# ScalarE issues the weights' transfers into ten slots, v is split and loaded a head sooner with its maximum pinned, and heads take even shares of the queued products

## The chip, the cores and the metric

One NeuronCore of a Trainium2 chip runs the whole program. TensorE (PE) multiplies, PEld is its weight load, VectorE (DVE) and ScalarE (ACT) do the elementwise work, GpSimd (POOL) helps them, SyncE (SP) issues transfers. All of them run in their own order and wait for each other through semaphores. The metric is the device time of one execution in microseconds (us); lower is better.

## The reference

Eight batches of eight attention heads with a decay on the scores, then a two-layer product with a hard swish between (`_attn_ref`, `_moe_ref`, cut):

```python
scores = (1/8) * q @ k.T                       # q, k, v: 8 x 8 x 576 x 64
cum = cumsum(log(clip(f, 1e-4, 1)))
scores = where(causal, -1e9, scores + cum[:, None] - cum[None, :])
attn = exp(scores - max); attn = attn / (sum(attn) + 1e-9)
x = (attn @ v), heads side by side             # 4608 x 512
h = x @ w_in                                   # w_in: 512 x 2048
out = (h * clip(h + 3, 0, 6) / 6) @ w_out      # w_out: 2048 x 512
```

The weights come as 64-bit floats; the kernel reads them as pairs of 32-bit integers.

## The kernel before

**Heads.** The list VH holds the order of the attention work: four A entries (two heads each, the first 256 rows of batch 0), eight B entries (the other rows of batch 0, one head each), then 56 F entries (one head each, batches 1 to 7). In A and B the scores are exponentiated into `pf` (L567); in F each row's maximum is taken by DVE (`pp` and `MF`, L619), ACT exponentiates (L631) and splits into two f16 parts in `ring`, and a transposing transfer brings them into `pT`. `av` multiplies by v into `pav`; `x_move` transposes the result into `xT`.

**Products.** A tile is 512 rows of x. `h_unit` makes `ph` (L781 to L783, three f16 products for one precise one) and from it, over `r` (ACT L791, DVE L794), `gT` (L795, L796). `out_unit` makes `po` (L803 to L805) and stores `o`. These units stand in a list, `units`; `done` appends a tile when its last head is done, and `fill`, called eight times a head, takes units off it as long as its credit lasts. The credit grows by `rates[0]`: 0.6 in B, 0.45 in batch 1, 1.02 in later batches. One tile costs about 64 credits.

**Weights.** Each of w_in and w_out comes in 16 chunks of 512 KB. A chunk is loaded into a slot (`w_load`, L237, on SP's queue), decoded into f32 (`w_decode`: ACT L250, DVE L251 and L252) and its squares summed (ACT L256); the slot is then free. After that a scale is made and the chunk is split into two f16 parts: w_in over ACT L283, TensorE (`low`, L286 and L287) and ACT L288, w_out over ACT L283 and DVE L294. w_in uses up to six slots (three `ring` buffers, three in the unused end of `w2`), five chunks ahead; w_out uses the three `ring` buffers. `both` takes the decoding of w_in and then of w_out in steps, W_RATE of them a head.

**v.** The f32 copy `vst` of one batch's v is loaded in three transfers (`load_v`, L359 and L360), its largest magnitude is reduced on DVE in two halves (`vm`, L365, in `v_scale`), a scale follows, and `v_split` makes the f16 parts of two heads at a time (ACT L396, DVE L397). The load of the next batch comes at head 6 of a batch, the maximum at head 7, the splits of a batch at head 7 of the one before and at heads 1, 3 and 5.

**Order.** The layer below the kernel (Tile) puts the instructions of each engine into one fixed order, from the order of the code and its own timeline of the program; only `tc.keep_in_program_order` and `tc.issue_after` bind it. On the chip each engine runs its order and waits at the first instruction whose semaphores are not there. A transfer announces its landing on one of eight semaphores (DMAHW0 to DMAHW7) which all transfers of the program take in turn, whichever engine issues them; a transfer waits until the one eight places before it has landed, so eight at most are under way.

Of the kernel before, what the change touches and what calls it, by code (L numbers as in the profile page):

```python
# [13 lines left out]
I32 = mybir.dt.int32  # L14
# [6 lines left out]
def kernel(  # L21
# [10 lines left out]
    nc = tc.nc  # L32
# [13 lines left out]
    NFC = DFF // P  # L46
    TT = 512
# [34 lines left out]
    NQK, NL, NST = 3, 2, 3  # L82
    W_RATE = (8, 5, 4)
    H_COST = 1.05
    F_RATE = (0.6, 0.45, 1.02)
    PIN = 0
    PIN0 = 1
    LOW_W = 0
    W_GAP = 5
# [5 lines left out]
    QA = 256  # L95
    CA = QA // P
    VH = [("A", g) for g in range(NPAIR)] + [("B", n) for n in range(H)]
# [3 lines left out]
    NSP = 3  # L101
    PL_POOL = ((3, ), ())
    NAT = ((1, 4, 0), (2, 3))
    B0_POOL = ((0, 0), (1, 1))
    W_AHEAD = (4, 5)
    W_ORDER = 0
    POOL_REST = ((0, 0, 0, 0), (0, 0, 0, 0))
    PIN_V = 1
# [22 lines left out]
    vst = cpool.tile([P, NCH, VR], F32, name="vst")  # L131
# [4 lines left out]
    xT = [cpool.tile([P, NCC, 2, TT // P, 2, 64], F16, name=f"xT{i}") for i in range(3)]  # L136
# [7 lines left out]
    def v_parts(b):  # L144
        return v0 if b == 0 else [vst[:, 0:3], vst[:, 3:]]
# [86 lines left out]

    def w_load(i, k, slots):
        src, x, _ = w_chunk(i, k)
        with pinned() if PIN or i == 0 and k < 8 else nullcontext():
            if wide:
                nc.sync.dma_start(slots[k % len(slots)], src.bitcast(I32))  # L237
            else:
                nc.sync.dma_start(x, src)

    def w_decode(i, k, slots):

# [51 lines left out]
            nc.vector.scalar_tensor_tensor(lo, x, sc, hi, op0=ALU.mult, op1=ALU.subtract)  # L294

    def w_in_work():
        first, ahead = W_AHEAD
        for k in range(first):
            w_load(0, k, slots_in)
        yield  # L300
        for k in range(first, ahead):
            w_load(0, k, slots_in)
        for j in range(NG):
            ks = range(j * NCC, (j + 1) * NCC)
            for k in ks:
                if k + ahead < NW:
                    w_load(0, k + ahead, slots_in)
                w_decode(0, k, slots_in)
                yield
            pm = w_gram(ks) if GRAM[j] else w_sum(ks[0], ks[-1] + 1)  # L310
            yield
            yield from pow2_scale(pm, S1 + j, I1 + j, f"w0{j}")
            eye = None
            if PE_LOW[j]:
                eye = p2.tile([P, DM], F32, tag="o", name=f"eye{j}")[:, 0:P]
                nc.vector.tensor_scalar(
                    eye, identf, scol(S1 + j), -1.0, op0=ALU.mult, op1=ALU.mult
                )
            for k in ks:
                w_split(0, k, scol(S1 + j), eye)  # L320
                yield
            w_in_done.append(j)

    def w_out_work():
        n = len(slots_out)
        for k in range(n):
            w_load(1, k, slots_out)
        yield

        for k in range(NW):  # L330
# [13 lines left out]
        for k in range(NW):
            w_split(1, k, scol(SW2 + k // NG))
            yield


    def load_v(b):
        src = vS[b]  # L350
        lo, hi = v_parts(b)
        with pinned() if PIN_V else nullcontext():
            if b == 0:
                nc.sync.dma_start(lo, src[0:3 * P].rearrange("(c p) e -> p c e", p=P))
                nc.sync.dma_start(hi[:, 0], src[3 * P:4 * P])
                nc.sync.dma_start(hi[:64, 1], src[4 * P:S])
            else:
                for p in (0, 64):
                    nc.sync.dma_start(vst[p:p + 64, 0], src[0:64])  # L359
                nc.sync.dma_start(vst[:, 1:], src[64:].rearrange("(c p) e -> p c e", p=P))  # L360

    def v_scale(b):
        pm = p2.tile([P, 2], F32, tag="pm", name=f"vm{b}")
        for i, t in enumerate(v_parts(b)):
            nc.vector.tensor_reduce(  # L365
                pm[:, i:i + 1], t.rearrange("p c (h e) -> p (c h) e", e=D + 1)[:, :, 0:D],
                axis=AX.XY, op=ALU.max, apply_absolute_value=True,
            )
# [466 lines left out]
    dec = decay()  # L835
    w_in_q = w_in_work()
    w_out_q = w_out_work()
    w_in_done = []

    def both():  # L840
        yield from w_in_q
# [34 lines left out]

    units = []

    credit, rates = [0.0], [1.0]

    def w_step():
        with tc.high_priority(offset=-LOW_W):
# [2 lines left out]
    def fill(k):  # L885
        credit[0] += k * rates[0]
        while credit[0] >= 1 and units:
            with tc.high_priority(offset=-LOW_M):
                r = next(units[0], 0)
            if r == 0:  # L890
                units.pop(0)
            else:
                credit[0] -= r
        credit[0] = min(credit[0], 1.0)

    def one(*a):
        yield from moe_tile(*a)

    def done(v):
        kind, n = VH[v]  # L900
        if kind == "A":
            if n == NPAIR - 1:
                units.append(one(0, 0, QA))
            return
        b, h = divmod(n, H)
        if h == H - 1:
            units.append(one(b, QA if b == 0 else 0, TT))
            if b == B - 1:
                units.append(one(B))

    prev = None
    pend_x = None
    vq = v_scale(0)
    for i, (kind, n) in enumerate(VH):
        b, h = divmod(n, H)
        if kind == "A":
            b = h = 0
        wn = W_RATE["ABF".index(kind)]
        rates[0] = F_RATE[0] if kind == "B" else F_RATE[min(b, 2)]
        ahead = i + 2 < NV  # L920
        if i + 3 < NV:
            load_x(i + 3)
        if ahead:
            load_c(i + 2)
# [24 lines left out]
        fill(1)  # L949
        if pend_x is not None:  # L950
            x_move(pend_x)
            done(pend_x)
            pend_x = None
        if front:
            natural(i + 2, 0)
# [18 lines left out]
            v_split(n // 2)  # L974
        fill(1)
        prev = (i, ph)
    rates[0] = 1.0
    av(*prev)
    fill(4)
# [40 lines left out]
```

## Time and profile before

| | |
|---|---|
| median of three runs | 1084.57 us (1083.75 to 1087.27) |
| the profiled execution | 1083.28 us, its span 1081.5 us |
| PE busy | 1010.1 us, 93% of the span |
| DVE, ACT, POOL busy | 719.7, 610.1, 413.1 us |
| TensorE clock granted, mean | 0.982 |
| transfers | 133.74 MB, 124 GB/s in the mean |

Five stages can be told by ACT's exponentials: A (to 65.2 us, where the first B head's exponential starts), B (to 133.1 us, where the last one's second half starts), the first F heads with the splits of w_out (to 190 us), the rest of batch 1 and the start of batch 2 (to 290 us), batches 2 to 7 (to 893 us), and last the products that are left. In the rows of the profile a number, a duration, an engine and a line stand first, then written tile, arrow, read tile; in brackets is the idle time of the engine before it and what ended that.

### The profile page before, as it was taken

How to read it: one execution, taken by the hardware profiler on the slowest of the kernel's cores; microseconds unless marked ns; L12 is line 12 of the kernel's file. 1: busy time of each engine (PE TensorE's matmuls, PEld its weight loads, DVE VectorE, ACT ScalarE, POOL GpSimd, SP SyncE). 2: the span in 40 equal slices, each digit the busy share in tenths (PEclk: the TensorE clock that was granted, in tenths of full speed). 3: DMA queues.
4: the chain of work that ended last, by engine and by line, in shares of the span. 5: the costliest groups of instructions: out<-in, count | busy, mean ns of one | idle time of the engine just before them, and what ended most of it. 6: DMA issues, size and time to landing. Idle time of an engine off the chain costs nothing.

```text
span 1081.5 us, 20281 instructions
## 1 busy us (share of the span) xinstructions
PE 1010.1 (93%) x7074; PEld 577.4 (53%) x7074; DVE 719.7 (67%) x1887; ACT 610.1 (56%) x1285; POOL 413.1 (38%) x505
## 2 busy tenths in 40 slices
PE   2799977988999999999999989999999999999998
PEld 2567854755555555555555545555555555444443
DVE  7869899876885688468865795689668841510520
ACT  4778656845764577356754674477447841621520
POOL 7344455335434445444544444454445420000000
PEclk9989989999999999999999999999999999999999
DMA  8866547767756666667576856675666651000001
GB/s 258 277 172 194 150 105 134 179 127 150 156 114 141 140 146 118 137 129 164 108 139 138 164 113 130 146 166 114 128 140 128 106 112 46 1 10 30 1 1 39
DMA packets 261650, 133.74 MB, mean 124 GB/s; under 512 B 229444, under 2 KB 231036, under 8 KB 261548
## 3 DMA queue, kind: packets, MB, share of 16 engines
q1 hardware_dynamic: 261548, 132.45, 54.7%
q8 instruction: 56, 0.92, 0.3%
q14 instruction: 46, 0.38, 0.1%
HBM read 47.93 MB, written 9.73 MB: 53 GB/s over the span
## 4 chain that ended last, share of the span: by engine, by line
PE 64%; DVE 12%; DMA 9%; issue 5%; ACT 5%; SPq 2%; POOL 2%; DVEq 0%; POOLq 0%; ACTq 0%
PE po L803 10%; PE po L804 10%; PE po L805 10%; PE ph L781 7%; PE ph L782 7%; PE ph L783 7%; DMA vst<-in_vS_dram 3%; PE pn L611 3%; PE pn L608 2%; DVE pp L619 2%; DVE ring L648 2%; DMA T<-TK 1%; DVE gT L796 1%; DMA w<-in_w_in_dram 1%; DVE r L794 1%
## 5 line engine op out<-in xcount | busy, mean ns | idle before, releaser
L781 PE MATMUL ph<-xT,w 128*128 128x512 f16 (+1 forms) x640 | 231.2, 363 | 14.5 <-DVE r L794 9.1
L782 PE MATMUL ph<-xT,w 128*128 128x512 f16 (+1 forms) x640 | 230.2, 363 | 0.0
L783 PE MATMUL ph<-xT,w 128*128 128x512 f16 (+1 forms) x640 | 230.0, 363 | 0.0
L631 ACT ACTIVATE pp<-pp,nb 128x192 f32<-128x192 f32 x280 | 138.5, 552 | 148.8 <-DVE nb L625 145.8
L804 PE MATMUL po<-w,gT 128*128 128x512 f16 x576 | 216.3, 381 | 6.1 <-DVE w L294 6.1
L805 PE MATMUL po<-w,gT 128*128 128x512 f16 x576 | 215.9, 381 | 0.0
L803 PE MATMUL po<-w,gT 128*128 128x512 f16 x576 | 213.6, 381 | 1.1 <-ACT o L814 0.8
L648 DVE TENSOR_TENSOR ring<-pp,ring 128x128 f16<-128x128 f32 (+2 forms) x216 | 131.5, 622 | 84.1 <-ACT ring L645 83.2
L791 ACT ACTIVATE r<-ph,bias_r,SC 128x256 f32<-128x256 f32 (+7 forms) x272 | 144.4, 570 | 28.6 <-PE ph L783 27.9
L794 DVE SCALAR_TENSOR_TENSOR r<-r,ph 128x512 f32<-128x512 f32 (+1 forms) x160 | 100.1, 627 | 88.9 <-ACT r L791 88.6
L458 POOL TENSOR_TENSOR T<-ST,T 64x576 fp32r<-64x576 f32 (+1 forms) x68 | 101.2, 1488 | 143.2 <-DMA T<-TK 133.4
L619 DVE CUSTOM_DVE_ANT_0 pp<-pn,W 128x192 f32<-128x192 f32 x280 | 122.9, 482 | 20.6 <-PE pn L611 16.6
L796 DVE TENSOR_TENSOR gT<-r,gT 128x512 f16<-128x512 f32 (+1 forms) x160 | 118.3, 743 | 27.4 <-ACT gT L795 26.6
L795 ACT CAST gT<-r 128x512 f16<-128x512 f32 (+1 forms) x160 | 91.8, 575 | 75.9 <-DVE r L794 75.8
L608 PE MATMUL pn<-TK,TQ 68*128 68x192 f32 x336 | 124.1, 383 | 5.8 <-issue 5.0
L611 PE MATMUL pn<-T,T 128*128 128x192 f32 x336 | 113.5, 368 | 4.3 <-POOL T L458 4.3
L645 ACT CAST ring<-pp 128x192 f16<-128x192 f32 x280 | 112.9, 452 | 0.0
L455 POOL TENSOR_TENSOR T<-ST,TQ 64x576 fp32r<-64x576 f32 (+2 forms) x68 | 97.6, 1435 | 24.8 <-PE pn L611 18.2
L654 POOL TENSOR_TENSOR ring<-pp,ring 128x128 f16<-128x128 f32 x96 | 61.5, 641 | 105.5 <-ACT ring L645 83.7
L782 PEld LDWEIGHTS <-w 128*128 128x128 f16 x640 | 62.7, 99 | 65.8 <-issue 20.9
L805 PEld LDWEIGHTS <-gT 128*128 128x128 f16 x576 | 56.8, 99 | 74.9 <-issue 13.7
L781 PEld LDWEIGHTS <-w 128*128 128x128 f16 x640 | 63.1, 99 | 62.2 <-issue 14.3
(136 smaller groups left out, 1703.4 us busy)
## 6 DMA issues: line engine op xcount, KB each, us to landing
ST<-in_qk_dram SPq DMA_DIRECT2D x64, 288.0 KB
T<-TK SPq DMA_DIRECT2D x64, 144.0 KB
out_dram<-o SPq DMA_DIRECT2D x36, 256.0 KB
ring<-in_w_out_dram SPq DMA_DIRECT2D x16, 512.0 KB
T<-TQ SPq DMA_DIRECT2D x56, 144.0 KB
vst<-in_vS_dram SPq DMA_DIRECT2D x7, 1040.0 KB
ring<-in_w_in_dram SPq DMA_DIRECT2D x9, 512.0 KB
w<-in_w_in_dram SPq DMA_DIRECT2D x7, 512.0 KB
```

Of the source, the lines that this page charges most:

```text
L608: nc.tensor.matmul(dst, TQ[i][0:D + 4, qs], TK[i][0:D + 4, a:e], start=True, stop=False)
L611: nc.tensor.matmul(dst, T7[j][:, qs], T1[j][:, a:e], start=False, stop=True)
L619: nc.vector.tensor_tensor_reduce(pp[:r, w:w + kw], pn[:r, o:o + kw], W[:r, 4 * P + r - kw:4 * P + r], 1.0, -3.0e38, ALU.add, ALU.max, accu ...
L631: nc.scalar.activation(x_, x_, AF.Exp, bias=nb[:r, e0 + x:e0 + x + 1], scale=0.125)
L648: eng.tensor_tensor(hl[:r, a:a + c * P], pp[:r, at[c] + 64:at[c] + kw], hl[:r, h0[c] + 64:h0[c] + kw], op=ALU.subtract,)
L781: nc.tensor.matmul(ph, w1[0][:, cc, fs_], xh, start=(cc == 0), stop=False)
L782: nc.tensor.matmul(ph, w1[0][:, cc, fs_], xl, start=False, stop=False)
L783: nc.tensor.matmul(ph, w1[1][:, cc, fs_], xh, start=False, stop=(cc == NCC - 1))
L791: nc.scalar.activation(r[:, a:e], ph[:, a:e], AF.Relu, bias=bias_r, scale=scol(A1 + NG * b + fc * NG // NFC))
L803: nc.tensor.matmul(po, gT[:, 0, fc, ts_], w2[:, fc, 0, :], start=(fc == 0), stop=False)
L804: nc.tensor.matmul(po, gT[:, 0, fc, ts_], w2[:, fc, 1, :], start=False, stop=False)
L805: nc.tensor.matmul(po, gT[:, 1, fc, ts_], w2[:, fc, 0, :], start=False, stop=(fc == NFC - 1))
```

## The change

`w_load` issues on ScalarE's queue instead of SP's, without pinning. The slots of w_out grow from three to five (two halves of `vst`), those of w_in from six to ten (these five, two in `xT[1]`, three in `w2`), and w_in is loaded as many chunks ahead as there are slots. `load_v` of later batches moves from head 6 to head 5, and `v_split` from heads 1, 3, 5 to 1, 2, 4; the maximum of later batches is kept in program order. A batch's tile enters the list one step later (`moved`). From batch 2 on the rate is no constant: `even` spreads the credits that are left, less a reserve of 8, over the heads until the next tile comes.

```diff
-    F_RATE = (0.6, 0.45, 1.02)
+    F_RATE = (0.6, 0.45)
-    W_AHEAD = (4, 5)
-    slots_out = [t[:, :] for t in ring]
-    slots_in = slots_out + [spare[:, (2 * h + 9) * CW:(2 * h + 11) * CW] for h in range(NSP)]
+    slots_out = [t[:, :] for t in ring] + [vsp[:, 2 * h * CW:2 * (h + 1) * CW] for h in range(2)]
+    slots_in = slots_out + [xsp[:, 2 * h * CW:2 * (h + 1) * CW] for h in range(2)]
+    slots_in += [spare[:, (2 * h + 9) * CW:(2 * h + 11) * CW] for h in range(NSP)]
 def w_load(i, k, slots):
-        with pinned() if PIN or i == 0 and k < 8 else nullcontext():
-                nc.sync.dma_start(slots[k % len(slots)], src.bitcast(I32))
+            nc.scalar.dma_start(slots[k % len(slots)], src.bitcast(I32))
 def w_in_work():
-        first, ahead = W_AHEAD
+        ahead = len(slots_in)
...
+                w_decode(0, k, slots_in)
                 if k + ahead < NW:
                     w_load(0, k + ahead, slots_in)
-                w_decode(0, k, slots_in)
 def v_scale(b):
-            nc.vector.tensor_reduce(
+            most = nc.vector.tensor_reduce(
...
+            if b:
+                tc.keep_in_program_order(most)
...
+    TILE = NFC * 2 * H_COST + TT // P * NFC // 2 * (2.0 - H_COST)
+    RESERVE = 8.0
+    def even(h):
+        heads = (1 - h) % H + 1
+        return min(max((left[0] - RESERVE) / (8 * heads), 0.5), 1.25)
...
-        rates[0] = F_RATE[0] if kind == "B" else F_RATE[min(b, 2)]
-        if b + 1 < B and h == 6:
+        if b and h in (1, 2, 4):
+            v_split(n // 2 + 1 if h > 1 else (n + 1) // 2)
+        if b + 1 < B and h == (5 if b else 6):
             load_v(b + 1)
-        if b and h % 2 == 1 and h < H - 1:
-            v_split((n + 1) // 2)
+        if moved is not None:
+            done(moved)
+            moved = None
+        rates[0] = F_RATE[0] if kind == "B" else F_RATE[b] if b < 2 else even(h)
...
             x_move(pend_x)
-            done(pend_x)
+            if VH[pend_x][0] == "F":
+                moved = pend_x
+            else:
+                done(pend_x)
```

The lines of the new code stand a few lines lower (L250 is L251 there, L567 is L570, L365 is L366).

**ACT at the start of the program.** `lf` is the logarithm from which the decay `cs` is made, `gT`, `ring`, `vst`, `xT` and `w` hold the slots or the decoded chunks. Before:

```order
L161 ACT_TABLE_LOAD
L161 ACTIVATE warm<-warm 1x1
L169 ACTIVATE lf<-fs 64x576
L170 ACT_TABLE_LOAD
L170 ACTIVATE warm<-lf 1x1
L250 ACTIVATE gT<-ring_123 128x512
```

Now, with the semaphores that each waits for:

```order
L238 DMA vst<-in_w_in_dram 128x1024
L238 DMA vst<-in_w_in_dram 128x1024 [waits DMAHW0_49]
L238 DMA xT_118<-in_w_in_dram 128x1024 [waits DMAHW1_49]
L238 DMA xT_118<-in_w_in_dram 128x1024 [waits DMAHW2_49]
L238 DMA w_115<-in_w_in_dram 128x1024 [waits DMAHW3_49]
L238 DMA w_115<-in_w_in_dram 128x1024 [waits DMAHW4_49]
L238 DMA w_115<-in_w_in_dram 128x1024 [waits DMAHW5_49]
L167 ACTIVATE lf<-fs 64x576 [waits DVE_49]
L251 ACTIVATE gT<-ring_124 128x512
```

Ten transfers stand before `lf` (three more ahead of these rows), and the last of them waits for the sixth transfer of the program, the third chunk.

**ACT at the first B head**, whose exponential is `pf_600`. Before:

```order
L288 ACTIVATE w_114<-low_447 128x512
L288 ACTIVATE w_114<-low_442 128x512
L256 ACTIVATE ring_125,wsum<-w_115 128x512
L567 ACTIVATE pf_600<-ps_0_601,bias_p 128x640
L256 ACTIVATE ring_123,wsum<-w_115 128x512
```

Now:

```order
L257 ACTIVATE vst,wsum<-w_115 128x512
L289 ACTIVATE w_114<-low_450 128x512
L257 ACTIVATE vst,wsum<-w_115 128x512
L289 ACTIVATE w_114<-low_445 128x512
L251 ACTIVATE w_115<-ring_123 128x512
L570 ACTIVATE pf_600<-ps_0_601,bias_p 128x640
```

Ahead of `pf_600` stand 32 decodings (all chunks of both weights) and 32 issues, where 19 decodings and no issue stood; ahead of the very first exponential, of the first A entry, 18 decodings where 6 stood.

**DVE at the maximum of a later batch's v**, batch 5's. Before:

```order
L619 ISA pp_1_6104,MF_109<-pn_1_6099,W 128x448
L619 ISA MF_109 128x1
L365 TENSOR_REDUCE vm_6760<-vst 128x1 x2
L648 TENSOR_TENSOR ring_123<-pp_0_6050,ring_123 128x128
L625 TENSOR_SCALAR nb_6040<-MF_109 128x2
```

Now (the second half of the maximum follows three heads later):

```order
L628 TENSOR_SCALAR nb_6110<-MF_108 128x3
L799 TENSOR_TENSOR gT<-r_3_0_6096,gT 128x512
L366 TENSOR_REDUCE vm_6673<-vst 128x1
L622 ISA pp_1_6175,MF_108<-pn_1_6170,W 128x320
L622 ISA MF_108 128x1
```

The two halves no longer stand together. The large part of the load stands on SP behind the transfers T of the following head (`T_102<-TQ_95`, `T_100<-TK_98`) and ahead of the transposing transfers of the head in which the first half of the maximum stands; no `v_split` of the old batch stands between head 4 and the load any more.

More of the change, by code (lines that the diff above doesn't have):

```diff
@@ L84 @@
     H_COST = 1.05
-    F_RATE = (0.6, 0.45, 1.02)
-    PIN = 0
+    F_RATE = (0.6, 0.45)
     PIN0 = 1
@@ L217 @@
     spare = w2.bitcast(I32).rearrange("p k a e -> p (k a e)")
-    slots_out = [t[:, :] for t in ring]
-    slots_in = slots_out + [spare[:, (2 * h + 9) * CW:(2 * h + 11) * CW] for h in range(NSP)]
+    vsp = vst.bitcast(I32).rearrange("p c e -> p (c e)")
+    xsp = xT[1].bitcast(I32).rearrange("p a h c l t -> p (a h c l t)")
+    slots_out = [t[:, :] for t in ring] + [vsp[:, 2 * h * CW:2 * (h + 1) * CW] for h in range(2)]
+    slots_in = slots_out + [xsp[:, 2 * h * CW:2 * (h + 1) * CW] for h in range(2)]
+    slots_in += [spare[:, (2 * h + 9) * CW:(2 * h + 11) * CW] for h in range(NSP)]
     def w_chunk(i, k):
@@ L234, in w_load @@
         src, x, _ = w_chunk(i, k)
-        with pinned() if PIN or i == 0 and k < 8 else nullcontext():
[L236 to L239, printed above, removed]
+        if wide:
+            nc.scalar.dma_start(slots[k % len(slots)], src.bitcast(I32))
+        else:
+            nc.scalar.dma_start(x, src)
     def w_decode(i, k, slots):
@@ L296, in w_in_work @@
     def w_in_work():
-        first, ahead = W_AHEAD
-        for k in range(first):
+        ahead = len(slots_in)
+        for k in range(ahead):
             w_load(0, k, slots_in)
         yield
-        for k in range(first, ahead):
-            w_load(0, k, slots_in)
         for j in range(NG):
@@ L331, in w_out_work @@
             w_decode(1, k, slots_out)
+            decoded.append(k)
             if k + n < NW:
@@ L351, in load_v @@
         lo, hi = v_parts(b)
+        assert b == 0 or len(decoded) == NW
         with pinned() if PIN_V else nullcontext():
@@ L837 @@
     w_out_q = w_out_work()
-    w_in_done = []
+    w_in_done, decoded = [], []
     def both():
@@ L877, with queue @@
     units = []
-    credit, rates = [0.0], [1.0]
+    credit, rates, left = [0.0], [1.0], [0.0]
+    TILE = NFC * 2 * H_COST + TT // P * NFC // 2 * (2.0 - H_COST)
+    RESERVE = 8.0
+    def queue(unit, columns):
+        units.append(unit)
+        left[0] += TILE * columns / TT
+    def even(h):
+        heads = (1 - h) % H + 1
+        return min(max((left[0] - RESERVE) / (8 * heads), 0.5), 1.25)
     def w_step():
@@ L893, in fill @@
                 credit[0] -= r
+                left[0] -= r
         credit[0] = min(credit[0], 1.0)
@@ L902, in done @@
             if n == NPAIR - 1:
-                units.append(one(0, 0, QA))
+                queue(one(0, 0, QA), QA)
             return
@@ L906, in done @@
         if h == H - 1:
-            units.append(one(b, QA if b == 0 else 0, TT))
+            queue(one(b, QA if b == 0 else 0, TT), TT - QA if b == 0 else TT)
             if b == B - 1:
-                units.append(one(B))
+                queue(one(B), TT)
     prev = None
-    pend_x = None
+    pend_x = moved = None
     vq = v_scale(0)
@@ L951 @@
             x_move(pend_x)
-            done(pend_x)
+            if VH[pend_x][0] == "F":
+                moved = pend_x
+            else:
+                done(pend_x)
             pend_x = None
@@ L976 @@
         prev = (i, ph)
+    if moved is not None:
+        done(moved)
     rates[0] = 1.0
```

## The prediction

> **What bounds the kernel now.** I read the page's head first, then the busy times of five stages and the tail, then in each stage what TensorE waited for.
>
> ```profile
> span 1081.5 us, 20281 instructions
> PE 1010.1 (93%) x7074; PEld 577.4 (53%) x7074; DVE 719.7 (67%) x1887; ACT 610.1 (56%) x1285; POOL 413.1 (38%) x505
> ```
>
> TensorE is busy for 1010.1 of 1081.5 us, and the change neither adds nor removes a matmul. So the time can only move by TensorE's idle time, 71.4 us in all, or by making new idle time. The stages (columns: busy us and count of PE, PEld, DVE, ACT, POOL, then the clock, the transfer engines' busy share, GB/s):
>
> ```profile
> 0.00:65.20 65.20, 35.52 (x148) 26.39 (x149) 47.74 (x148) 39.31 (x82) 35.29 (x51) 0.90 0.82 249
> 65.20:133.10 67.90, 66.25 (x501) 53.91 (x501) 57.62 (x153) 49.98 (x108) 28.91 (x31) 1.00 0.59 178
> 133.10:190.00 56.90, 43.59 (x348) 28.79 (x347) 56.20 (x153) 35.70 (x76) 33.78 (x33) 0.94 0.58 116
> 190.00:290.00 100.00, 90.59 (x753) 58.99 (x752) 77.45 (x220) 63.71 (x144) 40.49 (x50) 0.95 0.71 148
> 290.00:893.00 603.00, 590.16 (x4418) 325.01 (x4417) 434.34 (x1147) 365.92 (x791) 274.60 (x341) 0.99 0.65 134
> 893.00:1081.50 188.50, 184.02 (x916) 84.35 (x913) 46.39 (x71) 55.47 (x91) 0.00 (x0) 1.00 0.06 18
> ```
>
> Idle TensorE time by stage: 29.7 us in A, 1.7 in B, 13.3 with the splits of w_out, 9.4 up to 290 us, 12.8 in batches 2 to 7, 4.5 in the tail. A is bound by what feeds it (transfers 82% busy), B by TensorE, the third stage by DVE (56.20 of 56.90), all later ones by TensorE with gaps. What TensorE waited for from 290 to 893 us (total, times, longest):
>
> ```profile
> PE ph L781 <- DVE r L794: 8.1, 5, 3.2
> PE ph L781 <- DMA xT<-xhl: 4.7, 3, 2.2
> ```
>
> These two rows are the whole 12.8 us of that stage. The first one's origin, at the largest gap:
>
> ```profile
> 612.45 2.08 SPq L359 DMA_DIRECT2D vst<-in_vS_dram  x2
> 614.58 0.58 SPq L360 DMA_DIRECT2D vst<-in_vS_dram  x1
> 621.22 2.88 DVE L365 TENSOR_REDUCE vm<-vst 128x1 f32<-128x1536 f32 x2 [4.16 <-DMA vst<-in_vS_dram]
> 626.22 0.41 PE L781 MATMUL ph<-xT,w 128*128 128x512 f16 x1 [3.23 <-DVE r L794]
> ```
>
> DVE stands still for 4.16 us at the maximum of v, because the load was issued only at 614.58, then works 2.88 us at it, and `r` (L794), which frees a `ph` buffer, is queued behind: 7.04 us of blocked DVE cost TensorE 3.23 us.
>
> **Part 1, the load and the maximum of v (a gain).** The load moves from head 6 to head 5, and the splits that read the old `vst` are over by head 4. So it waits only for its place on SP, behind the next head's T transfers. In the trace these were issued a head earlier:
>
> ```profile
> 604.77 0.59 SPq L454 DMA_DIRECT2D T<-TK  x1
> 616.03 0.47 DVE L619 CUSTOM_DVE_ANT_0 pp<-pn,W 128x320 f32<-128x320 f32 x1
> 614.58 6.52 DMA vst<-in_vS_dram
> L365 DVE TENSOR_REDUCE vm<-vst x14: 1208/1480/1753, 124.1 to 731.6; 128x1 f32<-128x1536 f32 x7, 128x1 f32<-128x1024 f32 x7
> DVE vm L365 <- DMA vst<-in_vS_dram: 16.0, 6, 4.2
> ```
>
> (The third row is from the chain that ended last.) Issued at 605.4 us and 6.52 us under way, the load would be there at 611.9. The first half of the maximum now stands ahead of the second half of the scores, the row at 616.03, so it would be wanted about 4 us later. And the halves stand three heads apart, which blocks DVE for 1.75 and 1.21 us at a time. I take 7.6 of the 8.1 us; the ends are 0 and -8.1. What is late next is nothing on TensorE: units of the tile are still queued. The splits at heads 1, 2 and 4 are as many as before and cost nothing, as long as units are queued to cover them.
>
> **Part 2, the later queueing and the even rate (a gain).** The 4.7 us are a tile's first product at the head of TensorE's queue while its `xT` is still being transposed:
>
> ```profile
> 477.29 5.03 SPq L755 DMA_TRANSPOSE xT<-xhl  x4
> 483.56 0.38 PE L781 MATMUL ph<-xT,w 128*128 128x512 f16 x1 [1.94 <-DMA xT<-xhl]
> ```
>
> At a rate of 1.02 and eight fills a head, eight heads take 65 credits, and a tile has 64: the list is empty when the next tile comes, so its first product comes at once. Now the tile enters one step later and 8 credits of the old one are kept, about 10 us of products (64 credits are 384 matmuls, at the tail's 184.02 us for 916 some 77 us). I take 4.4 of 4.7 us; the ends are 0 and -4.7. In program order this moves some 75 matmuls from the heads into the tail. That costs nothing: there TensorE is as busy (184.02 of 188.50). Parts 1 and 2 together: -12.
>
> **Part 3, ScalarE issues the weights (a loss in A).** Removed from SP are 32 issues, added to ACT are 32:
>
> ```profile
> L237 SPq DMA_DIRECT2D ring<-in_w_out_dram x16: 323/420/1287, 32.8 to 110.7; - x16
> L237 SPq DMA_DIRECT2D ring<-in_w_in_dram x9: 327/432/534, 2.0 to 44.8; - x9
> L237 SPq DMA_DIRECT2D w<-in_w_in_dram x7: 328/430/742, 3.5 to 44.2; - x7
> ```
>
> At a median of 0.43 us that is 13.8 us. No row shows ACT issuing: it is between nothing (issued while an activation runs) and 13.8. ACT's work itself moves forward: 32 decodings stand ahead of the first B exponential where 19 stood. One costs the step between two L250:
>
> ```profile
> 4.32 0.68 ACT L169 ACTIVATE lf<-fs 64x576 f32<-64x576 f32 x1 [2.08 <-DVE fs L167]
> 10.25 0.65 ACT L250 ACTIVATE gT<-ring 128x512 f32<-128x512 f32 x1
> 10.81 0.61 ACT L256 ACTIVATE ring<-gT 128x512 f32<-128x512 f32 x1
> 11.42 0.65 ACT L250 ACTIVATE gT<-w 128x512 f32<-128x512 f32 x1
> 65.19 0.79 ACT L567 ACTIVATE pf<-ps,bias_p 128x640 f32<-128x640 f32 x1
> 133.09 0.74 ACT L567 ACTIVATE pf<-ps,bias_p 128x576 f32<-128x576 f32 x1
> ```
>
> From 10.25 to 11.42 is 1.17 us, and 13 of them 15.2 us. ACT's 39.3 us of stage A become 39.3 + 15.2 + 13.8 = 68.3. And `lf`, at 4.32 us now, stands behind an issue that waits for the third chunk (with the q and k ahead of it some 2.4 MB, 7.5 us at the 321 GB/s below, and 2 to begin with: 9.5 to 10.5 us): 6 us in which ACT computes nothing. Together 74.5, with some idling at waits 76: the first B exponential comes at 76 us in place of 65.2, **+11**.
>
> Bytes bound this from the other side. By then all of the weights (32 x 0.524 = 16.8 MB) and about 5.4 MB else have landed: 2.5 of q and k (4 x 256 and 5 x 288 KB), 1.2 of v, 1.3 of T copies, 0.4 of f and the decay; 22.2 MB in all. Sizes, queue, and the most that the trace moved in 20 us:
>
> ```profile
> ring<-in_w_out_dram SPq DMA_DIRECT2D x16, 512.0 KB
> ST<-in_qk_dram SPq DMA_DIRECT2D x64, 288.0 KB
> T<-TK SPq DMA_DIRECT2D x64, 144.0 KB
> v<-in_vS_dram SPq DMA_DIRECT2D x1, 780.0 KB
> q1 hardware_dynamic: 261548, 132.45, 54.7%
> 20.00:40.00 20.00, 15.94 (x62) 12.56 (x63) 16.95 (x51) 12.29 (x26) 8.14 (x9) 1.00 0.98 321
> ```
>
> So 2 + 22.2/0.321 = 71 us at best, and 91 at A's mean of 249 GB/s: +6 to +26, and nothing or a gain is excluded, since the first B exponential stands behind the last chunk. I stay near the lower end, since ten slots keep more under way than six. [...]
>
> Who waits for ACT then: `pf`, so `pav`, so every later pair. The small transfers on SP (TK<-cs, TQ<-mr) no longer stand behind weights in one queue, but they take the same eight semaphores: TK<-cs now waits for the sixth and the eighth chunk, which lands at about 18 us (5.1 MB at 321 GB/s, and 2) where TK<-cs had landed at 12.8. That delays the first scores, inside the 11 us as long as ACT ends last.
>
> **Part 4, what the earlier decoding gives back.** In B 13 decodings are gone from ACT and DVE. TensorE has 1.7 us of idle time there, and its busy time is not all at its peak: I take -3; the ends are 0 and -8 (half of ACT's 15.2). In the third stage four splits of w_out stand ahead of the first F head's DVE rows where none stood:
>
> ```profile
> L294 DVE SCALAR_TENSOR_TENSOR w<-w,SC x16: 733/738/1609, 139.3 to 191.4; 128x512 f16<-128x512 f32 x16
> PE po L804 <- DVE w L294: 6.1, 5, 1.8
> ```
>
> 4 x 0.74 = 3.0 us less in a stage that DVE fills: -3, the ends 0 and -6.1, the whole of TensorE's wait for the splits. From 190 to 290 us and in the tail I see no change (0, give or take 3: the 9.4 us of gaps there come from `pT` and POOL's T, which only shift).
>
> **Sum.** +11 - 3 - 3 - 12 = -7. The profiled execution took 1083.28 us, 1.8 over its span and 1.3 under the median of the runs; against it 1076.3, against the median **1077.6, told as 1077**.
>
> **Rivals.**
>
> *ACT becomes the bound of A (slower).* ACT's queue is in order, and the first exponential of all now stands behind 18 decodings where 6 stood, the first B one behind all 32. If the chunks come at the stage's mean of 249 GB/s, the 91 us above hold: +26 - 18 = +8, so 1092. Against it speaks that 321 GB/s were seen. It decides once the first B exponential comes later than 83 us (+18, all the gains); slower by over 0.3% from 86.
>
> *Freed SP (faster still).* TensorE waited in A for small transfers behind the weights in SP's one queue:
>
> ```profile
> PE pn L484 <- DMA TK<-cs: 12.8, 1, 12.8
> PE ps L548 <- DMA TQ<-mr: 7.4, 2, 4.3
> ```
>
> If on their own queue they pass the weights and ACT's issues hide beneath activations, A ends at the byte bound (+6), and B and the third stage gain their upper ends: +6 - 8 - 6.1 - 12 = -20, so 1064. Against it: `lf` and TK<-cs wait for chunks as said, and TensorE fills B. [...]
>
> *The wait for v only moves.* If the pinned maximum still meets an unlanded load, only part 2's 4.4 us remain of the 12: 11 - 6 - 4.4 = +0.6, so 1085. Against it stand the 4 us above.
>
> **How the numbers follow.** Chances: forecast 0.50 (its own range 1069 to 1083, A between +5 and +17), ACT-bound A 0.22, freed SP 0.15, moved wait 0.13. About 0.3%, or 3.3 us, is what a measurement of this kernel can tell from no change. The forecast gives 0.44 to faster and 0.06 to no change, freed SP 0.15 to faster, the moved wait 0.02, 0.08 and 0.03, the ACT-bound A 0.05 to no change and 0.17 to slower: 0.61, 0.19, 0.20. The range takes in the upper part of freed SP and the lower half of ACT-bound A: 1063 to 1090.
>
> **What would show it.** Parts 1 and 2: from batch 2 on no wait of `ph` for `r` or `xT` above 1 us, and DVE's wait at `vm` near 0 (16.0 us in all now). Part 3: the first B exponential at 76 us; at 71 the freed SP is right, at 86 or later the ACT-bound A. Part 4: B's last exponential about 65 us after its first (67.9 now), and fewer waits of `po` for the splits. I am wrong if A grows by over 18 us, or if the blocked DVE stays.

## The result, and the profile after

The changed kernel took 1110.70 us (median of 4 runs, 1105.52 to 1117.71) against 1084.16 us for the kernel before, beside it (4 runs): a ratio of 1.0249, 95% interval 1.0211 to 1.0287. It is 26.5 us slower. Forecast were 1077 us, 1063 to 1090, and a gain. Two executions of the experiments below, one of e11 (3634.70 us) and one of e16 (1096.73 us), were in a slow state and are left out of their rows.

The profiled execution took 1111.79 us. Its page's head, and its stages with the columns of the stage table of before; the borders are the first and last exponentials of B here, the later ones moved along with the work:

```profile
span 1110.0 us, 20272 instructions
PE 1015.7 (92%) x7074; PEld 581.0 (52%) x7074; DVE 729.3 (66%) x1887; ACT 611.6 (55%) x1285; POOL 413.1 (37%) x505
```
```profile
0.00:84.40 84.40, 37.48 (x152) 27.25 (x153) 64.33 (x173) 54.68 (x120) 37.92 (x54) 0.96 0.84 269
84.40:148.50 64.10, 64.10 (x497) 53.35 (x495) 40.85 (x128) 36.08 (x70) 26.91 (x30) 1.00 0.35 88
148.50:207.00 58.50, 46.11 (x335) 29.69 (x334) 52.14 (x145) 34.07 (x72) 33.18 (x31) 0.85 0.55 111
207.00:307.00 100.00, 90.81 (x801) 59.75 (x798) 82.96 (x228) 65.31 (x146) 46.62 (x55) 1.00 0.71 149
307.00:900.00 593.00, 571.65 (x4278) 316.71 (x4277) 441.14 (x1143) 363.68 (x787) 267.64 (x337) 0.99 0.64 134
900.00:1110.00 210.00, 205.57 (x1021) 94.23 (x1018) 47.84 (x74) 57.78 (x95) 0.80 (x1) 1.00 0.07 21
```

Length minus PE's busy time is its idle time: 46.9, 0.0, 12.4, 9.2, 21.4 and 4.4 us, 94.3 in all, where it was 29.7, 1.7, 13.3, 9.4, 12.8 and 4.5, together 71.4. Of the 28.5 us by which the span grew, 22.9 are idle time, nearly all of it in two places: +17.2 in stage A and +8.5 in batches 2 to 7. The other 5.6 us are busy time (1015.7 against 1010.1) with the same 7074 matmuls. Some 2.6 of them are the clock, by an estimate: the trace has stretches in which half of TensorE's clock was granted, TensorE was busy in them for 33.9 us where it had been 28.7, and half of the difference is 2.6. The mean granted clock over the span did not fall (0.983 against 0.982), and the other 3 us are not explained. The last stage holds 1021 recorded products where the tail held 916, so the products did move into the tail.

What TensorE waited for, over the whole run (total, times, longest), and VectorE's wait at the maximum of v:

```profile
PE pn L487 <- DMA TK<-cs: 24.1, 1, 24.1
PE ptm L502 <- DVE MC L493: 14.1, 3, 10.1
PE ph L784 <- DVE r L797: 14.0, 9, 5.3
PE pav L694 <- DMA pT<-ring: 13.0, 10, 3.7
PE ph L784 <- DMA xT<-xhl: 1.7, 1, 1.7
```
```profile
DVE vm L366 <- DMA vst<-in_vS_dram: 23.0, 4, 8.5
```

The first two rows are stage A: 12.8 and 3.1 us before. The waits for `xT` fell, as foretold, from 5.3 to 1.7 us. But `ph` waited 14.0 us for `r`, not less than the 9.1 of before, and VectorE stood 23.0 us at the maximum, not near 0 (16.0 before). The wait of `pav` for the transposes of `pT` more than doubled, to 13.0 from 5.6.

**The wait at the maximum.** The largest, by SP's, VectorE's and TensorE's rows, and the windows around it (columns as in the stage table):

```profile
622.80 1.13 SPq L360 DMA_DIRECT2D vst<-in_vS_dram  x2
624.03 0.54 SPq L818 DMA_DIRECT2D out_dram<-o  x1
624.66 7.04 SPq L758 DMA_TRANSPOSE xT<-xhl  x5
631.87 1.47 SPq L669 DMA_TRANSPOSE pT<-ring  x1
...
636.98 0.59 SPq L457 DMA_DIRECT2D T<-TK  x1
637.61 0.60 SPq L361 DMA_DIRECT2D vst<-in_vS_dram  x1
```
```profile
643.18 1.22 DVE L366 TENSOR_REDUCE vm<-vst 128x1 f32<-128x1024 f32 x1 [8.45 <-DMA vst<-in_vS_dram]
645.27 0.59 PE L784 MATMUL ph<-xT,w 128*128 128x512 f16 x1 [5.31 <-DVE r L797]
```
```profile
630.00:640.00 10.00, 9.96 (x84) 5.49 (x82) 3.60 (x13) 4.17 (x10) 0.46 (x2) 1.00 0.71 134
645.00:648.40 3.40, 3.13 (x9) 1.66 (x9) 2.64 (x7) 3.40 (x8) 1.84 (x2) 0.53 0.36 71
```

The two small pieces of v's load are issued at 622.80, the large one (L361) only at 637.61: a store of `o`, five transposes of `xT`, two of `pT` and the next head's small loads and T transfers stand in between. The order has the smaller half of the maximum early (its turn comes at 634.73, its start less its wait) and the larger half some 80 instructions later. So VectorE stands still for 8.45 us, `r` behind it comes late, and TensorE stops for 5.31 us. The last row shows a second price: in the 3.4 us after the stop the granted clock is 0.53, by an estimate some 1.6 us more (0.47 of 3.4).

**Stage A.** ScalarE's rows, its issues (ACTq) among them, then TensorE's and VectorE's:

```profile
5.50 0.34 ACTq L238 DMA_DIRECT2D vst<-in_w_in_dram  x1
6.32 4.39 ACTq L238 DMA_DIRECT2D xT<-in_w_in_dram  x2
10.74 3.58 ACTq L238 DMA_DIRECT2D w<-in_w_in_dram  x3
14.37 0.68 ACT L167 ACTIVATE lf<-fs 64x576 f32<-64x576 f32 x1 [11.73 <-DMA xT<-in_w_in_dram]
46.72 0.88 ACT L570 ACTIVATE pf<-ps,bias_p 128x768 f32<-128x768 f32 x1
84.36 1.42 ACT L570 ACTIVATE pf<-ps,bias_p 128x640 f32<-128x640 f32 x2
148.48 0.73 ACT L570 ACTIVATE pf<-ps,bias_p 128x576 f32<-128x576 f32 x1
```
```profile
24.11 2.04 PE L487 MATMUL pn<-TK,TQ 66*128 66x128 f32 x8 [24.11 <-DMA TK<-cs]
33.70 0.28 DVE L493 CUSTOM_DVE_ANT_0 junk<-pn,W 128x128 bf16<-128x128 f32 x1
36.22 0.27 PE L502 MATMUL ptm<-identr,MC 128*4 128x128 f32 x1 [10.07 <-DVE MC L493]
```

`lf` comes at 14.37 us, not 4.32: it stands behind ten issues, and the last six, at 5.50 to 14.32 us, wait on semaphores of earlier transfers. The first scores are there at 24.1 us, but VectorE gets to their maximum (`junk`) only at 33.70, because ten decodings of w_in stand ahead of it in its queue (4 before). The first exponential of all comes at 46.72 us (24.96 before), the first of B at 84.36 (65.19).

### The profile page after: what moved, and what is told of

Its sections match the earlier page's. It is cut to its first block, busy times and chain, and to the rows that moved or that the text cites. A ratio compares the mean times of both kernels' runs of the same rounds, so it can differ in the third digit from the quotient of the medians.

```text
span 1110.0 us, 20272 instructions
## 1 busy us (share of the span) xinstructions
PE 1015.7 (92%) x7074; PEld 581.0 (52%) x7074; DVE 729.3 (66%) x1887; ACT 611.6 (55%) x1285; POOL 413.1 (37%) x505
## 4 chain that ended last, share of the span: by engine, by line
PE 66%; DVE 11%; DMA 9%; ACT 5%; issue 5%; POOL 2%; SPq 1%; ACTq 0%; DVEq 0%; POOLq 0%
PE po L806 10%; PE po L807 10%; PE po L808 10%; PE ph L784 8%; PE ph L786 7%; PE ph L785 7%; DMA pT<-ring 3%; PE pn L614 3%; PE pn L611 3%; PE pav L705 2%; DVE pp L622 2%; DMA ST<-in_qk_dram 2%; DVE ring L651 2%; ACT pp L634 2%; DMA vst<-in_vS_dram 2%
## 5 line engine op out<-in xcount | busy, mean ns | idle before, releaser
L784 PE MATMUL ph<-xT,w 128*128 128x512 f16 (+1 forms) x640 | 226.9, 361 | 15.7 <-DVE r L797 14.0
L785 PE MATMUL ph<-xT,w 128*128 128x512 f16 (+1 forms) x640 | 226.2, 360 | 0.0
L786 PE MATMUL ph<-xT,w 128*128 128x512 f16 (+1 forms) x640 | 225.8, 359 | 0.0
L651 DVE TENSOR_TENSOR ring<-pp,ring 128x128 f16<-128x128 f32 (+2 forms) x216 | 138.2, 652 | 68.4 <-ACT ring L648 67.7
L622 DVE CUSTOM_DVE_ANT_0 pp<-pn,W 128x192 f32<-128x192 f32 x280 | 123.0, 481 | 23.1 <-PE pn L614 19.6
L611 PE MATMUL pn<-TK,TQ 68*128 68x192 f32 x336 | 126.7, 390 | 3.0 <-DVE MF L622 2.9
L458 POOL TENSOR_TENSOR T<-ST,TQ 64x576 fp32r<-64x576 f32 (+2 forms) x68 | 102.7, 1511 | 18.4 <-PE pn L614 12.7
L785 PEld LDWEIGHTS <-w 128*128 128x128 f16 x640 | 62.7, 98 | 70.0 <-issue 20.2
L786 PEld LDWEIGHTS <-w 128*128 128x128 f16 x640 | 62.7, 98 | 65.3 <-issue 7.8
L784 PEld LDWEIGHTS <-w 128*128 128x128 f16 x640 | 61.8, 98 | 58.6 <-issue 9.5
```

Of the source, the lines that this page charges most:

```text
L611: nc.tensor.matmul(dst, TQ[i][0:D + 4, qs], TK[i][0:D + 4, a:e], start=True, stop=False)
L622: nc.vector.tensor_tensor_reduce(pp[:r, w:w + kw], pn[:r, o:o + kw], W[:r, 4 * P + r - kw:4 * P + r], 1.0, -3.0e38, ALU.add, ALU.max, accu ...
L651: eng.tensor_tensor(hl[:r, a:a + c * P], pp[:r, at[c] + 64:at[c] + kw], hl[:r, h0[c] + 64:h0[c] + kw], op=ALU.subtract,)
L784: nc.tensor.matmul(ph, w1[0][:, cc, fs_], xh, start=(cc == 0), stop=False)
L785: nc.tensor.matmul(ph, w1[0][:, cc, fs_], xl, start=False, stop=False)
L786: nc.tensor.matmul(ph, w1[1][:, cc, fs_], xh, start=False, stop=(cc == NCC - 1))
```

## The experiments

Each kernel ran beside the kernel before; gains and losses in us are the ratio times the 1084 us of before, so that they can be added. "W" is the weights' part, "V" the v change, "E" the later queueing (`moved`) with the even rate.

| kernel | median us | ratio (95% interval) | us |
|---|---|---|---|
| e1 before + W | 1095.39 | 1.0106 (1.0074 to 1.0138) | +11.5 |
| e2 before + V | 1074.15 | 0.9891 (0.9854 to 0.9928) | -11.8 |
| e3 before + E | 1099.48 | 1.0138 (1.0108 to 1.0168) | +15.0 |
| e4 before + V + E | 1098.00 | 1.0136 (1.0107 to 1.0166) | +14.7 |
| e5 before + `moved` | 1090.29 | 1.0037 (1.0008 to 1.0066) | +4.0 |
| e6 before + even rate | 1099.71 | 1.0129 (1.0092 to 1.0166) | +14.0 |
| e8 before + V + `moved` | 1067.28 | 0.9834 (0.9798 to 0.9871) | -18.0 |
| e9 as e4, reserve 4 | 1082.29 | 0.9986 (0.9966 to 1.0006) | -1.5 |
| e15 as e4, reserve 0 | 1069.64 | 0.9874 (0.9838 to 0.9910) | -13.7 |
| e16 as e8, rate 1.08 | 1085.43 | 1.0014 (0.9986 to 1.0043) | +1.5 |
| e12 W, six and three slots | 1088.75 | 1.0066 (1.0036 to 1.0096) | +7.2 |
| e14 W, six and five slots | 1092.26 | 1.0094 (1.0064 to 1.0124) | +10.2 |
| e13 W, ten and three slots | 1104.72 | 1.0179 (1.0133 to 1.0224) | +19.4 |
| e10 W, issued by SP | 1104.44 | 1.0191 (1.0159 to 1.0223) | +20.7 |
| e11 W, `lf` behind four issues | 1104.06 | 1.0196 (1.0158 to 1.0234) | +21.3 |

### The parts one by one

e1 takes the hunks of `slots_in`, `w_load` and `w_in_work`; e2 those of `load_v`, `v_split` and `v_scale`; e3 those of `moved` and `even`; e4 is the changed kernel without the hunks of e1:

```diff
 e2
+            if b:
+                tc.keep_in_program_order(most)
...
+        if b and h in (1, 2, 4):
+            v_split(n // 2 + 1 if h > 1 else (n + 1) // 2)
-        if b + 1 < B and h == 6:
+        if b + 1 < B and h == (5 if b else 6):
             load_v(b + 1)
-        if b and h % 2 == 1 and h < H - 1:
-            v_split((n + 1) // 2)
```

> The kernel before with part 3 alone: ScalarE issues the weights, ten and five slots. Theory 1 (each part has its own cost): stage A loses what it lost in the changed kernel, first B exponential at 84 us against 65, TensorE's idle time up by about 17 us, the later stages give 3 back: 1084 + 17 = 1101 to 1104 us. Theory 2 (the late start costs everything, because the queued products slide into the tail): all 26.5 us of the loss are here, 1111. The prediction's sum for this part was +11 - 3 - 3 = +5, 1089.

> The kernel before with the v change alone: load at head 5, splits at heads 1, 2 and 4, the maximum pinned. Theory 1 (the pinned maximum fails only together with the even rate): here the load's pieces still follow one another on SP and the two halves of the maximum stand side by side on DVE, so DVE's wait at the maximum falls from 16 us to under 5 and 4 to 8 us are gained: 1076 to 1080 us. Theory 2 (pinning it is the loss by itself): the wait stays at 16 to 23 us and the time is 1084 to 1090.

> The kernel before with the later queueing and the even rates alone. Theory 1 (the even rate moves the large piece of v's load on SP behind the next head's small loads, 11 to 13 places after the small pieces): waits of ph for xT fall from 5.3 us to under 2, but DVE waits over 16 us at the maximum of v and ph for r more than the 9.1 us of before: 1084 to 1090 us. Theory 2 (the prediction: it only takes the waits for xT away): 1080 us, ph's wait for r unchanged.

> The changed kernel with the weights' transfers as before (SP, six and three slots). Theory 1 (the parts do not help each other: pin and even rate together put the half of the maximum ahead of its load): the idle time of batches 2 to 7 is as in the changed kernel, 21 us against 13, DVE waits some 23 us at the maximum, and the time is 1088 to 1094 us. Theory 2 (all of the loss is the weights): the prediction's 12 us of gain show, 1072.

W and V + E add up: 11.5 + 14.7 = 26.2 us, and the change cost 27.0 (1.0249). W cost less than the 17 to 20 us of theory 1. V gains 11.8 alone, more than its text had. E loses 15.0: its waits are those of theory 1, but the loss is larger than either theory gave, and so is that of e4. V and E put together do not give -11.8 + 15.0 = +3.2 but +14.7: the gain of V is lost where E is there. In e2 VectorE never waited for v of a later batch; in e3 and e4 it did (VectorE's row and TensorE's row of e3, then VectorE's of e4):

```profile
DVE vm L365 <- DMA vst<-in_vS_dram: 34.6, 7, 7.3
PE ph L781 <- DVE r L794: 24.1, 8, 6.9
```
```profile
DVE vm L365 <- DMA vst<-in_vS_dram: 26.7, 4, 8.0
```

### Which half of E

e5 keeps the old rates and queues a tile one step later; e6 has the even rate and queues as before; e8 is e5 with V:

```diff
 e5 and e8
             x_move(pend_x)
-            done(pend_x)
+            if VH[pend_x][0] == "F":
+                moved = pend_x
+            else:
+                done(pend_x)
...
+        if moved is not None:
+            done(moved)
```

> The kernel before with one half of part 2: a tile is queued one step after its transposes are issued, the rates stay. The pieces of v's load follow one another on SP as before. Theory 1 (the loss of part 2 lies in the even rate): the waits of ph for xT (5.3 us) go, 2 to 5 us are gained, 1079 to 1082 us. Theory 2 (the later queueing leaves TensorE without products at a tile's border): 1088 us or more.

> The kernel before with the other half of part 2: the even rate with a reserve of 8, tiles queued as before. Theory 1: here the last piece of v's load stands 11 to 13 places later on SP, DVE waits some 35 us at the maximum, and most of the 15.9 us of part 2 are lost: 1094 to 1100 us. Theory 2 (it takes both halves): 1084 to 1090 us.

> Placeholder of the same kernel as the third run of the first group: one look, to see how far its idle times repeat; 1095 to 1101 us.

> The kernel before with the v change and the later queueing, rates as before: the candidate for the batches. Theory 1: the gains add, 1074 - 4 = 1070 us. Theory 2: the queueing adds nothing to the v change, 1074.

The even rate is the loss: e6 loses as much as e3. The third text belongs to one more execution of e3's kernel, on another chip; it took 1108.72 us, outside what was expected, with the same waits (38.2 us at the maximum, 25.2 for `r`), so a single execution can lie 0.8% off. The later queueing alone is a small loss, +4.0 (0.9 to 7.2), in the range of theory 2 and not of theory 1. But a lack of products does not show: TensorE's waits for `xT` are gone, and those for `r` grew instead, from 9.1 us, behind a maximum for which VectorE waited 19.6 us (16.0 before):

```profile
PE ph L781 <- DVE r L794: 15.8, 7, 4.3
```

With V, which takes that wait away, the later queueing gains 18.0 - 11.8 = 6.2 us. The intervals of e2 and e8 overlap a little, but the waits agree: V alone leaves TensorE waiting 8.7 us for `xT` (e2), and 2.3 are left in e8. In e8 batches 2 to 7 have no gap left (window of its page, columns as above):

```profile
300.00:900.00 600.00, 599.42 (x4477) 327.56 (x4476) 442.60 (x1133) 361.78 (x779) 265.53 (x334) 1.00 0.63 132
```

This version beats both kernels, by 1.66% (1.29 to 2.02%) the one before.

### What in the even rate costs

At a reserve of 8 the order has the last of v's three pieces 11 to 13 transfers behind the others and, with V, the halves of the maximum some 80 instructions apart; at a reserve of 4 or 0 the pieces follow one another and the halves stand 7 instructions apart or closer (all of this in the loads of batches 4 to 7):

```diff
-    RESERVE = 8.0
+    RESERVE = 4.0     # e9; 0.0 in e15
```
```diff
 e16
-    F_RATE = (0.6, 0.45, 1.02)
+    F_RATE = (0.6, 0.45, 1.08)
```

> The v change and part 2 with a reserve of 4 in place of 8, weights as before. At 4 the order puts the last piece of v's load right behind the others on SP again, and the halves of the maximum side by side, as with the old rates. Theory 1 (the loss of the even rate is the late piece and the blocked VectorE): no wait at the maximum, ph waits for r under 3 us, 1066 to 1070 us as with the v change and the later queueing. Theory 2 (the products kept back thin out the heads and are missing there): half of the loss stays, 1080 to 1086 us.

> The v change and part 2 with a reserve of 0. Theory 1 (each product kept back for later is missing as cover for the transposes of pT): the waits of pav for pT, 14.7 us at a reserve of 4, fall under 8, and the time comes near the 1067 us of the fixed rate: 1066 to 1073. Theory 2 (evening the rate is the loss, whatever is kept back): 1078 to 1084 us as at a reserve of 4.

> The v change and the later queueing with a rate of 1.08 instead of 1.02, the other direction from a reserve. Theory 1 (products are worth most in the heads, as cover): the same or better than at 1.02, 1062 to 1068 us. Theory 2 (a list that is empty sooner brings the waits for xT back): ph waits for xT over 5 us, 1070 to 1076.

Two steps can be told apart. From 8 to 4 the blocked VectorE goes (no wait at the maximum beyond the 1.2 us of the first batch, `ph` for `r` 1.1 us in place of 15.8 in e4) and 16.2 us are won, but not all: theory 2 of e9 held, half stayed. This step changes the order and the products kept back together, so the 16.2 us are not all shown to be the blocked VectorE. From 4 to 0, where the order of the load stays, another 12.2 us come back. TensorE's waits for `pT` in e9 and in e15:

```profile
PE pav L693 <- DMA pT<-ring: 14.7, 11, 3.4
```
```profile
PE pav L693 <- DMA pT<-ring: 7.5, 6, 2.0
```

So 7.2 of those 12.2 us, read from one execution each, are waits for the transposes. That the products kept back are what had covered them is theory 1 of e15, and its two numbers came out (7.5 us, 1069.64); the other 5 us are not explained. With nothing kept back the even rate can't be told from the fixed one (0.9874 and 0.9834, the intervals overlap). More is not better either: at a rate of 1.08, 19.5 us are lost against 1.02. Neither theory of e16 holds: the time is above both, and the waits for `xT` did not come back (2.3 us), which theory 2 had said. The row that grew most is `ph` for `r`, 12 short ones:

```profile
PE ph L783 <- DVE r L796: 9.0, 12, 1.9
```

That is 8 us of the 19.5 (1.0 us in e8), and the waits for `pT` are 3.3 more (7.8 against 4.5 us); the rest, and why `r` comes late here, is not explained.

### The weights

e12 is the nearest to a change of the issuer alone: its slots are the six and three of before (the first sentence of its text has that wrong), but like all kernels with W it loads as many chunks of w_in ahead as there are slots, six for five, and decodes a chunk before it issues the next load. e10 has the ten and five slots and SP as issuer, with the first eight loads pinned as before; e11 is e1 with four issues ahead of `lf`; e13 and e14 deepen only one of the weights. The edits of e10 and e11, against e1:

```diff
 e10
-            nc.scalar.dma_start(slots[k % len(slots)], src.bitcast(I32))
+            nc.sync.dma_start(slots[k % len(slots)], src.bitcast(I32))
 e11
-        for k in range(ahead):
+        for k in range(4):
             w_load(0, k, slots_in)
         yield
+        for k in range(4, ahead):
+            w_load(0, k, slots_in)
+        yield
...
     next(dec)
+    next(w_in_q)
     load_c(0)
```

> The kernel before with ten and five slots, the transfers issued by SP. Theory 1 (the logarithm of the decay waits on ScalarE behind ten issues): lf runs at 4.3 us as before, no issue stands on ScalarE, and part 3's 11.8 us shrink to 0 to 4: 1084 to 1088 us. Theory 2 (32 decodings ahead of the first B exponential are the loss, whoever issues): 1094 to 1097. Theory 3 (SP's queue makes the small transfers wait behind ten chunks): TK<-cs lands later than 20 us, 1095 or more.

> Part 3 alone with one change: four issues ahead of lf on ScalarE instead of ten, the other six behind it. Theory 1: lf runs at 5 to 6 us instead of 14.4, TK<-cs lands some 8 us sooner, the first exponential of all comes at 36 to 39 us instead of 46.7, and the loss falls by about 8 us: 1084 to 1089 us. Theory 2 (the decodings): the first B exponential stays at 80 us or later, 1092 to 1096.

> Part 3 with the slots as before (three for both weights, without the spare room in w for w_in): ScalarE issues, but only three chunks are ahead. Theory 1: with three issues lf runs at 5 us, fewer decodings stand ahead of the first B exponential, and the time is 1084 to 1090 us. Theory 2 (a chunk that is issued only after a decoding on the same engine comes late): the weights end later, 1095 us or more.

> Part 3 alone with ten slots for w_in and three for w_out. Theory 1 (VectorE's and ScalarE's queues: each chunk that is ahead is decoded ahead of the first scores): 18 decodings stand ahead of the first exponential as with ten and five slots, 27 ahead of the first B exponential instead of 32; at 1.3 us each the first B exponential comes at 76 to 78 us instead of 83.2, and the time is 1089 to 1093 us. Theory 2 (only the second weights' depth counts): as with six and three slots, 1086 to 1090.

> Part 3 alone with six slots for w_in and five for w_out. Theory 1: 28 decodings ahead of the first B exponential, so that it comes at 76 to 79 us, 1089 to 1094 us. Theory 2 (only the ten slots of w_in, with lf behind ten issues, count): first B exponential by 72 us, 1085 to 1090.

ScalarE's row of the first B exponential in e12, e14, e13, e10 and e11:

```profile
68.50 0.78 ACT L566 ACTIVATE pf<-ps,bias_p 128x640 f32<-128x640 f32 x1
```
```profile
75.65 0.78 ACT L568 ACTIVATE pf<-ps,bias_p 128x640 f32<-128x640 f32 x1
```
```profile
76.74 0.79 ACT L569 ACTIVATE pf<-ps,bias_p 128x640 f32<-128x640 f32 x1 [0.71 <-PE ps L551]
```
```profile
79.62 1.42 ACT L569 ACTIVATE pf<-ps,bias_p 128x640 f32<-128x640 f32 x2
```
```profile
83.67 0.79 ACT L571 ACTIVATE pf<-ps,bias_p 128x640 f32<-128x640 f32 x1
```

Decodings ahead of it on ScalarE, by the order: 19 before, 23, 28, 27, 31 and 32 in these five, 32 in the change. The start of B rises with that count, from 65.2 us at 19 to 84.4 at 32, 1.5 us for each; the five lie up to 3.3 us under that line. In e11 `lf` runs at 7.14 instead of 14.43 us and TK<-cs is issued 5 us sooner, but the first exponential comes only 1.6 us sooner, 45.16 against 46.72: the decodings ahead of it on VectorE and ScalarE hold it, not `lf`. Theory 1 of e11 fell, and where ScalarE issues, the depth is what moves the start of B.

With SP as issuer the same depth is paid in another place. In e10 `lf` runs at 4.33 us and VectorE comes to the first maximum at 23.18 us, ten sooner than in the change. But the wait for TK<-cs ended only at 20.7 us (12.8 before), as theory 3 of e10 had it, and the first TQ<-mr, whose data were there at 25.5, was issued at 31.41, behind six chunks and four small transfers on SP (22.55 to 30.50), and had landed at 38.03. So e10 does not tell theory 2 from theory 3; theory 1 fell.

The total does not follow the start of B alone, and e10, e11 and e13 came out 7 us and more above the times that theories 1 and 2 gave them. e1 and e11 both reach B near 83.5 us and end 9.8 us apart by the ratios; B in e11, then in e1:

```profile
83.67:156.29 72.62, 72.50 (x504) 59.13 (x503) 44.40 (x136) 36.48 (x70) 23.04 (x28) 0.89 0.29 73
```
```profile
83.24:149.04 65.80, 64.83 (x497) 53.68 (x496) 42.88 (x132) 35.88 (x69) 27.31 (x31) 1.00 0.37 94
```

TensorE is busy nearly throughout in both; the granted clock is 0.89 in e11 and 1.00 in e1. The stretch is 6.8 us longer in e11, which is most of the 9.8. The trace shows where the clock fell: in e11 TensorE stood still for 3.03 us just ahead of B, and behind that stop only half of the clock was granted for 17.1 us:

```profile
82.17 1.12 PE L287 MATMUL low<-gT,eye 128*128 128x512 f32 x2 [3.03 <-ACT w L289]
83.30:100.40 17.10, 17.10 (x56) 12.07 (x54) 6.66 (x28) 8.18 (x16) 6.29 (x9) 0.50 0.23 54
```

In e1 no stop of TensorE between 75 and 149 us is longer than 0.7 us. The mean granted clocks of all executions agree: 0.984 to 0.986 in the four of e1, 0.974, 0.978 and 0.984 in e11 (1108.37, 1104.06 and 1099.96 us, the faster the higher), and 0.973 to 0.975 in the four of e10. In e13 (0.975 to 0.980) busy time is only 1.1 of the 10.0 us by which its profiled execution is longer than e1's; what makes its idle time, at fewer decodings than in e1, is open.

## Why the prediction was wrong

By parts the forecast was +5 for the weights (parts 3 and 4) and -12 for parts 1 and 2; measured were +11.5 (e1) and +14.7 (e4). So the larger error lies in parts 1 and 2. Both signs of being wrong that the prediction named came: A grew by more than 18 us, and the blocked DVE stayed.

- **The reading of before** held in the main: the time moved by TensorE's idle time, 22.9 of 28.5 us. It left out that busy time can grow too, 5.6 us here, some 2.6 of them by the estimate above the clock.
- **Part 1, the load and the maximum of v**: right on its own. Forecast 7.6 us, measured 11.8 (7.8 to 15.8, e2), with the wait at `vm` gone. In the change it failed in the step "Issued at 605.4 us and 6.52 us under way, the load would be there at 611.9 ... wanted about 4 us later". The place behind the T transfers was read off the new order, but its time was taken from before's trace; in the changed kernel the large part was issued at 637.61 and the maximum's turn came at 634.73, so the wait was not gone but 8.45 us long.
- **Part 2** was the largest miss. The step "In program order this moves some 75 matmuls from the heads into the tail. That costs nothing" failed: the reserve of 8 cost 14.7 + 13.7 = 28.4 us against a reserve of 0 (e4, e15), 12.2 for the first half and 16.2 for the second, and it undid part 1. Products that leave the heads are missing there, and the constant moved v's load on SP; the prediction put both at nothing. The 75 are not worked out there; the tail of the changed kernel has 105 more. The later queueing gave 6.2 us on top of V, where 4.4 were taken: that mechanism was right beside V, and alone it lost 4.0.
- **Part 3**: A was forecast at +11 and came at +19.2 (84.36 against 65.19). The step that failed is the sum itself, "ACT's 39.3 us of stage A become 39.3 + 15.2 + 13.8 = 68.3": it adds up ScalarE only. Its term for the decodings was right, 39.3 + 15.2 = 54.5 against 54.7 us busy; but ScalarE was idle for 29.7 of the 84.4 us, where the sum left 21.5 for issues and waits. The decodings also went ahead of the scores on VectorE, 64.33 us busy where it was 47.74, and the scores passed through both queues in turn. `lf` was 4 to 5 us later than the 9.5 to 10.5 taken, which by e11 mattered little. Issuing on ScalarE was over-priced at 13.8: e12 with all 32 issues lost 7.2 us in all, four more decodings among them. The bytes did not hold A either: behind `lf` ScalarE waited 2.3 us for chunks. (That ten slots keep more under way than six is not so: eight transfers at a time are the limit that the order sets, and in the trace eight were issued by 3.55 us and the ninth at 5.50, when the first had landed. A's mean went from 249 to 269 GB/s.)
- **Part 4**: B took 64.1 us, 3.8 less, near the 3 forecast: 1.7 of idle time and 2.15 of TensorE's busy time (66.25 to 64.10), with a granted clock of 1.00 in both. The third stage gave 0.9 us of idle time, not 3: `po` still waited 6.8 us for the splits (6.1 before), and the clock there was 0.85 against 0.94. The sum of the part held better than its terms: in e1 A grew by 18.1 us and the median by 11.8 (1095.39 against 1083.59), so some 6 came back later, as forecast.
- **The rivals.** The start of B at 84.4 lay short of the 86 of the ACT-bound A, but a stage bound by decodings was nearer than the forecast. "The wait for v only moves", given 0.13, is what happened to v of batches 4 to 7, at a higher price than the one it was given, since a wait that moves can also grow. None of the rivals put a loss on part 2, so none gave the measured time. Of "freed SP" one half is seen: TensorE's wait for TQ<-mr (7.4 us) is gone in the changed kernel, and in e10, with the weights on SP, it is 13.7:

```profile
PE ps L550 <- DMA TQ<-mr: 13.7, 3, 11.0
```

From its issue the first TQ<-mr took 6.6 us in e10 (31.41 to 38.03) and at most 3.9 in the kernel before (18.35 to 22.20, TensorE's next product), both with the weights on SP, and at most 2.3 in the changed kernel (37.20 to 39.53). What holds a transfer between its issue and its landing no row shows. The rest of the longest wait in e10, 11.0 us, lies before the issue. The shorter wait gained nothing, because the scores waited for VectorE next (`ptm` for MC, 14.1 us).

## What to carry to other kernels

Work that is moved ahead goes ahead on every engine that it touches: add up each in-order queue that the waiting chain passes, not only the one that the change names. A position that is read off a new order has no time until it is set against the new order's own neighbours; and a constant that only holds work back can reorder transfers far from it, so try it at zero. Products that fill gaps are worth most where there is something to cover, and a part that gains alone can lose all of it beside another, so time parts alone and together.

## What the runs showed of the hardware

Some stops of TensorE were paid again after them. In the changed kernel TensorE stopped four times for over 2 us in batches 2 to 7, for 2.7 to 5.3 us each, and after every one of them only half of the clock was granted for 3.4 us. The products of `ph` started 0.43 us apart in such a stretch (645.23 to 648.64) and 0.22 us apart behind it. Behind the stop of 5.31 us the granted clock was 0.53 for 3.4 us (645.0 to 648.4), and behind the next one of 3.66 us 0.63, since there the half clock began only at 757.9:

```profile
757.00:760.40 3.40, 3.40 (x16) 2.37 (x14) 3.32 (x6) 2.60 (x6) 0.72 (x1) 0.63 0.18 36
```

In e8, without such stops, batches 2 to 7 ran at 1.00. The length of a stop alone does not tell whether the half clock follows. In the kernel before, half of the clock came behind a stop of 2.17 us and the full clock stayed behind one of 2.22 us:

```profile
403.75 0.38 PE L781 MATMUL ph<-xT,w 128*128 128x512 f16 x1 [2.17 <-DVE r L794]
404.57:407.98 3.41, 3.41 (x10) 1.40 (x8) 3.38 (x10) 2.32 (x5) 0.35 (x1) 0.50 1.25 148
592.68 0.38 PE L781 MATMUL ph<-xT,w 128*128 128x512 f16 x1 [2.22 <-DMA xT<-xhl]
592.70:600.00 7.30, 7.30 (x65) 4.41 (x65) 5.26 (x16) 4.61 (x9) 0.94 (x2) 1.00 0.90 162
```

Behind e11's stop of 3.03 us the half clock lasted 17.1 us, in all of which the records have TensorE busy. What brought the full clock back there no run shows.

The last five issues ahead of `lf` waited for semaphores and took 8.0 us on ScalarE (6.32 to 14.32). The 22 behind `lf` took 0.33 to 0.45 us each in the changed kernel, and 16 of them ran while an activation did, as at 57.18 us:

```profile
57.05 0.65 ACT L251 ACTIVATE w<-ring 128x512 f32<-128x512 f32 x1
57.18 0.34 ACTq L238 DMA_DIRECT2D vst<-in_w_out_dram  x1
57.61 0.88 ACT L570 ACTIVATE pf<-ps,bias_p 128x768 f32<-128x768 f32 x1
```
